# Sparse attention before a bilinear feed-forward: from half-array to whole-array matmuls on TensorE

## The chip, the cores and the metric

One core of a Trainium2 chip. The time is device microseconds of that core; "before" and "after" are the two kernels, each run several times. Profiled spans are about 1 to 2 us shorter than the timed runs. In the views PE is TensorE, PEld its weight loads, DVE VectorE, ACT ScalarE and POOL GpSimd; PSUM holds TensorE's results.

## The reference, cut to what matters

```python
B, H, S, D = 8, 8, 576, 64
scores = q @ k.T / 8                       # per batch and head
mask_local   = (0 <= i - j) & (i - j < 32)              # heads 0..3
mask_strided = (0 <= i - j) & (i % 32 == j % 32)        # heads 4..7
attn = softmax(where(mask, scores, -1e9))
x = (attn @ v).transpose(0, 2, 1, 3).reshape(4608, 512)
out = ((x @ w_a) * (x @ w_b)) @ w_out      # d_ff = 1536
```

## The kernel before

The feed-forward takes the tokens in 9 tiles of 512. A tile is 16 groups: 12 of `ffn_ab` (8 matmuls of 512 columns each) and 4 of `ffn_y` (12 each). The attention of batch 0 comes first; the attention of batch t+1 is cut into slots, one behind each group of tile t. An attention matmul uses half of the array, by rows or by columns, and two stand side by side. The steps of a batch have short names: T transposes q and k of a pair of heads (Tq and Tk apart in the kernel after), S makes scores, exp and mask, V is P times v, and X, in the kernel after alone, transposes x. The number is the pair for T and X (0 to 3), and half of a pair's queries for S and V (0 to 7).

```python
# transposes: two heads, each into half of the columns
for r in range(R):
    for hh in range(2):
        nc.tensor.transpose(tp[64*hh:64*hh+64, r, :], src[:, 2*cc+hh, r, :], ident[:n, :n])
# scores: each head in half of the rows
nc.tensor.matmul(st[:M, hh, i*n:(i+1)*n], lhsT=kT[d0:d0+64, c, k0:k0+M], rhs=qT[d0:d0+64, c, q0:q0+n], ...)
# denominators by ones, P times v, each head in half of the columns
nc.tensor.matmul(dn[64*hh:64*hh+64, :W], lhsT=ones[:M], rhs=p[:M, hh], ...)
nc.tensor.matmul(o[64*hh:64*hh+64, i*n:(i+1)*n], lhsT=vt, rhs=p[:M, hh, i*n:(i+1)*n], ...)
nc.scalar.activation(ln, dn[:, :W], ACT.Ln)
nc.scalar.activation(rc, ln, ACT.Exp, scale=-1.0)
nc.vector.tensor_mul(x[...], o[:, :W], rc)       # written straight into xT
# ... (cut)
```

TensorE's, GpSimd's and the DMA queue's order is the program's; ACT's and VectorE's order is made by a scheduler.

The softmax here doesn't subtract the row's maximum and nothing guards it: scores larger than these inputs give would overflow.

## Time and profile before

| | before |
|---|---|
| time, median | 375.7 us (375.3 to 376.4) |
| profiled span | 374.7 us |
| first feed-forward matmul | 25.21 us |
| tile 0 (with batch 1's attention) | 42.56 us |
| a later tile with attention | 39.95 us |
| the last tile, without | 31.08 us |

The times of tiles are differences between the starts of their first feed-forward matmuls. Read TensorE's order of time first: it carries 93% of the chain that ended last, so every microsecond of it is in the time. The prediction below shows those lines. One line that it does not show is of use later. It is from TensorE's timeline at the start of tile 1; the bracket says how long the engine had been idle and who ended that:

```profile
69.36 0.38 PE L254 MATMUL mm<-xT,wa_sb 128*128 128x512 bf16 x1 [0.77 <-DVE xT L232]
```

Three matmuls of that group start at 67.77 and the fourth should follow at 68.42; it starts 0.94 us late, since x's last quarter was late.

### The profile page before, as it was taken

To read this page: it belongs to the slowest core of one execution; us is meant where nothing else is said; L and a number is where in the kernel's file an instruction comes from. 1 tells how busy PE (TensorE), PEld (TensorE's weight loads), DVE (VectorE), ACT (ScalarE), POOL (GpSimd) and SP (SyncE) were. 2 spreads that over 40 slices of the span, in tenths; PEclk is the share of its full clock that TensorE was granted. 3 is DMA by queue.
4 is the path that set the end of the run, shared out by engine and by line. 5 is a ranking of instruction groups with operands and counts; after the bars stand their busy time and mean duration, and the time that the engine had idled before them with its cause. 6 is when DMAs were issued, how large, how long until landed. Compare 5 with 4: busy or idle time off the path is not lost.

```text
span 374.7 us, 7708 instructions
## 1 busy us (share of the span) xinstructions
PE 358.7 (96%) x3217; PEld 173.8 (46%) x3217; DVE 169.7 (45%) x299; ACT 178.6 (48%) x347; POOL 52.3 (14%) x72
## 2 busy tenths in 40 slices
PE   2789999999999999999999999999999999999995
PEld 2544454455444544444444544554445444444442
DVE  2653652465426652556245643655255513312421
ACT  1563764466526652666246643766166623312320
POOL 7833540013001110103000300000000000000000
PEclk9999999999999999999999999999999999999999
DMA  7999999845644194229414843000200020011002
GB/s 114 155 194 197 205 191 191 177 66 37 98 117 65 8 100 117 53 40 103 93 56 66 72 81 99 2 2 19 94 2 3 1 86 28 0 58 56 0 30 84
DMA packets 51730, 29.59 MB, mean 79 GB/s; under 512 B 28400, under 2 KB 47088, under 8 KB 51696
## 3 DMA queue, kind: packets, MB, share of 16 engines
q0 software_dynamic: 46512, 19.67, 43.2%
q1 hardware_dynamic: 5184, 9.44, 6.9%
q8 instruction: 25, 0.41, 0.4%
q14 instruction: 9, 0.07, 0.1%
HBM read 39.31 MB, written 9.44 MB: 130 GB/s over the span
## 4 chain that ended last, share of the span: by engine, by line
PE 93%; DMA 2%; POOL 1%; ACT 1%; DVE 1%; issue 1%; DVEq 0%; POOLq 0%
PE mm L254 52%; PE mm L265 25%; PE sm L166 5%; PE st L194 4%; PE sm L213 4%; PE sm L220 2%; DMA vl<-in_v_dram 2%; POOL k L116 0%; DVE y_sb L271 0%; POOL msl L73 0%; ACT rc L226 0%; DVE xT L232 0%; ACT ln L224 0%; POOL q L116 0%; PE mm L166 0%
## 5 line engine op out<-in xcount | busy, mean ns | idle before, releaser
L259 DVE TENSOR_TENSOR pf<-a_sb,mm 128x512 bf16<-128x512 f32 x108 | 74.3, 688 | 89.9 <-PE mm L254 89.9
L254 PE MATMUL mm<-xT,wa_sb 128*128 128x512 bf16 x432 | 113.6, 386 | 0.8 <-DVE xT L232 0.8
L254 PE MATMUL mm<-xT,wb_sb 128*128 128x512 bf16 x432 | 111.9, 382 | 0.0
L258 ACT COPY a_sb<-mm 128x512 f32<-128x512 f32 x108 | 63.2, 585 | 70.2 <-PE mm L254 70.2
L265 PE MATMUL mm<-wo_sb,pf 128*128 128x512 bf16 x432 | 96.3, 379 | 0.0
L254 PEld LDWEIGHTS <-wb_sb 128*128 128x128 bf16 x432 | 42.6, 99 | 52.9 <-issue 2.9
L265 PEld LDWEIGHTS <-pf 128*128 128x128 bf16 x432 | 40.9, 98 | 47.9
L254 PEld LDWEIGHTS <-wa_sb 128*128 128x128 bf16 x432 | 36.4, 98 | 38.4 <-issue 1.7
L199 ACT ACTIVATE p<-st 128x576 bf16<-128x576 f32 (+1 forms) x64 | 40.7, 635 | 17.5 <-PE st L194 17.4
L224 ACT ACTIVATE ln<-sm 128x288 f32<-128x288 f32 x64 | 26.3, 410 | 29.5 <-PE sm L213 29.5
L269 ACT COPY y_sb<-mm 128x512 f32<-128x512 f32 x18 | 10.5, 585 | 56.3 <-PE mm L265 56.3
L271 DVE COPY y_sb<-mm 128x512 f32<-128x512 f32 x18 | 12.5, 692 | 52.9 <-PE mm L265 52.9
L232 DVE TENSOR_TENSOR xT<-sm,rc 128x288 bf16<-128x288 f32 x32 | 20.4, 639 | 28.4 <-ACT rc L226 27.8
L226 ACT ACTIVATE rc<-ln 128x288 f32<-128x288 f32 x64 | 28.3, 443 | 2.0
L172 ACT COPY qT<-sm 128x576 bf16<-128x576 bf16 x28 | 17.8, 637 | 13.9 <-PE sm L166 13.9
L194 PE MATMUL st<-qT,kT 64*72 64x72 bf16 (+1 forms) x448 | 21.1, 212 | 0.6 <-ACT p L199 0.5
L213 PE MATMUL sm<-p,ones 72*64 72x288 bf16 (+1 forms) x128 | 21.1, 327 | 0.3 <-DVE p L205 0.3
L229 DVE TENSOR_TENSOR xT<-sm,rc 128x288 bf16<-128x288 f32 x32 | 14.6, 458 | 14.2 <-ACT rc L226 12.5
L116 POOL DMA_DIRECT2D q<-in_q_dram x16 | 11.7, 730 | 58.4 <-PE sm L166 53.7
L213 PEld LDWEIGHTS <-ones 72*64 72x64 bf16 (+1 forms) x128 | 7.3, 110 | 24.6 <-issue 21.2
L166 PEld LDWEIGHTS <-q 72*64 72x64 bf16 (+1 forms) x448 | 11.2, 117 | 15.9 <-issue 8.9
L129 POOL DMA_DIRECT2D vl<-in_v_dram x8 | 11.6, 1454 | 45.9 <-PE st L194 45.4
(41 smaller groups left out, 177.8 us busy)
## 6 DMA issues: line engine op xcount, KB each, us to landing
out_dram<-y_sb SPq DMA_DIRECT2D x36, 256.0 KB, 2.0
q<-in_q_dram POOLq DMA_DIRECT2D x16, 288.0 KB, 6.8
k<-in_k_dram POOLq DMA_DIRECT2D x16, 288.0 KB, 7.9
vl<-in_v_dram POOLq DMA_DIRECT2D x7, 384.0 KB, 6.8
vs<-in_v_dram POOLq DMA_DIRECT2D x8, 288.0 KB, 5.8
wa_sb<-in_moe_w_a_dram POOLq DMA_DIRECT2D x4, 384.0 KB, 11.6
wb_sb<-in_moe_w_b_dram POOLq DMA_DIRECT2D x4, 384.0 KB, 11.7
wo_sb<-in_moe_w_out_dram POOLq DMA_DIRECT2D x4, 384.0 KB, 13.5
```

The lines of the kernel that those rows point to most:

```text
L166: nc.tensor.transpose(tp[64 * hh:64 * hh + 64, r, :], src[:, 2 * cc + hh, r, :], ident[:n, :n])
L172: nc.scalar.copy(o, i_)
L194: nc.tensor.matmul(st[:M, hh, i * n:(i + 1) * n], lhsT=kT[d0:d0 + 64, c, k0:k0 + M], rhs=qT[d0:d0 + 64, c, q0:q0 + n], start=True, stop=True)
L199: nc.scalar.activation(p[:M], st[:M, :, :W], ACT.Exp, scale=scale)
L213: nc.tensor.matmul(dn[64 * hh:64 * hh + 64, :W], lhsT=ones[:M], rhs=p[:M, hh], start=True, stop=True)
L224: nc.scalar.activation(ln, dn[:, :W], ACT.Ln)
L226: nc.scalar.activation(rc, ln, ACT.Exp, scale=-1.0)
L232: nc.vector.tensor_mul(dst, o[:, :W].rearrange("d (r p) -> d p r", r=4), rc.rearrange("d (r p) -> d p r", r=4))
L254: nc.tensor.matmul(ps_, lhsT=w[:, f // FC, kk, 128 * (f % FC):128 * (f % FC + 1)], rhs=xT[:, kk, TTOK * t:TTOK * (t + 1)], start=(kk == 0) ...
L258: nc.scalar.copy(a_sb, ab[0])
L259: nc.vector.tensor_mul(pf[:, f, :], a_sb, ab[1])
L265: nc.tensor.matmul(y, lhsT=pf[:, f, 128 * j:128 * (j + 1)], rhs=wo_sb[:, f, :], start=(f == 0), stop=(f == FD - 1))
```

## The change

Its intent: leave the array whole, so that it need not change its shape. k is loaded for both heads of a pair over 128 rows, and q stands in two tiles with the other head's half zeroed. P becomes the loaded operand, read 128 columns wide, and v with a 65th column of ones the moving one, so that the denominators come along and x comes out with queries on the partitions; it must then be transposed on TensorE. Local q and k are regrouped by GpSimd so that one transpose takes two heads (from batch 2 on).

```diff
-            for hh in range(2):
-                nc.tensor.transpose(tp[64*hh:64*hh+64, r, :], src[:, 2*cc+hh, r, :], ident[:n, :n])
+            nc.tensor.transpose(tv[:, r, :], perm_t[b, nm][:, r, 2*c:2*c+2, :], ident[:96, :96])   # b > 1
-                nc.scalar.copy(o, i_)
+            for j in range(2):
+                nc.scalar.copy(perm(qz_buf[b % 2][j][pr, c, :]), tv[pr])     # pr: half of the partitions
-    lhsT=kT[d0:d0+64, c, k0:k0+M], rhs=qT[d0:d0+64, c, q0:q0+n]
+    lhsT=kT[:, c, k0:k0+M],        rhs=qz[j][:, c, q0:q0+n]
-    dn: lhsT=ones[:M], rhs=p[:M, hh];  o: lhsT=vt, rhs=p[:M, hh, i*n:(i+1)*n];  Ln, Exp(-1), mul
+    o: lhsT=p[:M, j, i*n:i*n+128], rhs=vt   # 65 columns
+    nc.vector.reciprocal(rc, ov[:, :, :, D]);  nc.vector.tensor_mul(xn, ov[..., 0:D], rc)
+    def step_X(b, c):  # transposes of xn, nc.scalar.copy into xT
+    def perm_qk(b):
+        nc.gpsimd.tensor_copy(t.rearrange("p r h d -> p h r d"), nats[b, nm, False])
-pmm 4 banks, psm 2, pst 2
+pmm 3 banks, po 2 (one tile), ptp 1 (one tile), pst 2 (one tile)
+batch b's slots begin two groups before tile b-1; batch 1's begin after group 2 of tile 0,
+with two slots behind groups 3 and 12 (Tq0 then S0,Tk1; S6 then S7,X2)
# ... (cut: order of loads, clearing of buffers, last y in halves)
```

## The prediction

> **What bounds the kernel now.** I read the page first (engine shares, chain of work that ended last, costliest groups), then the timeline of TensorE in three stretches, then the sums over windows.
>
> ```profile
> PE 358.7 (96%) x3217; PEld 173.8 (46%) x3217; DVE 169.7 (45%) x299; ACT 178.6 (48%) x347; POOL 52.3 (14%) x72
> PE mm L254 52%; PE mm L265 25%; PE sm L166 5%; PE st L194 4%; PE sm L213 4%; PE sm L220 2%; DMA vl<-in_v_dram 2%; POOL k L116 0%; DVE y_sb L271 0%; POOL msl L73 0%; ACT rc L226 0%; DVE xT L232 0%; ACT ln L224 0%; POOL q L116 0%; PE mm L166 0%
> ```
>
> TensorE carries 93% of the chain, and no other engine is half busy. So I read TensorE's own order. One feed-forward group, one attention slot, a group, a slot:
>
> ```profile
> 156.70 1.03 PE L254 MATMUL mm<-xT,wb_sb 128*128 128x512 bf16 x4
> 157.66 0.31 PE L213 MATMUL sm<-p,ones 128*64 128x288 bf16 x2
> 157.80 0.29 PE L220 MATMUL sm<-p,vl 128*64 128x96 bf16 x6
> 158.03 0.30 PE L194 MATMUL st<-qT,kT 64*128 64x96 bf16 x6
> 158.26 1.04 PE L254 MATMUL mm<-xT,wa_sb 128*128 128x512 bf16 x4
> ...
> 162.53 0.45 PE L166 MATMUL sm<-ident,q 72*64 72x72 bf16 x16
> 162.81 0.43 PE L166 MATMUL sm<-ident,k 72*64 72x72 bf16 x16
> 163.18 1.04 PE L254 MATMUL mm<-xT,wa_sb 128*128 128x512 bf16 x4
> ```
>
> The first number is the start of a group, so differences of starts are what a group costs. In the last tile, which has no attention, feed-forward groups run back to back:
>
> ```profile
> 339.50 1.03 PE L254 MATMUL mm<-xT,wa_sb 128*128 128x512 bf16 x4
> ...
> 360.22 10.52 PE L265 MATMUL mm<-wo_sb,pf 128*128 128x512 bf16 x48
> ```
>
> That is 20.72 us for 96 matmuls, 215.8 ns each, so a tile of 144 costs 31.08 us. A tile with attention takes 39.95 us:
>
> ```profile
> 150.43:190.38 39.95, 39.95 (x385) 19.29 (x385) 19.57 (x34) 21.42 (x42) 4.98 (x6) 1.00 0.51 74
> ```
>
> Attention therefore costs 8.87 us of TensorE per batch, and that is what the change can shorten. Its anatomy: a group of four wb_sb matmuls starts at 156.70 and should be through at 157.56, but the slot starts at 157.66: 0.10 us lost. From 158.03 three pairs of 96 columns should take 3 x 0.0425 = 0.13 us, yet the feed-forward resumes 0.23 us later: 0.10 lost again; between 157.80 and 158.03 once more. Each loss falls where the array's shape changes (128\*128, 128\*64, 64\*128). The sequence of one batch has 33 such changes (2 for a slot of one kind of work, 3 for a slot of two): 33 x 0.10 = 3.3 us. The rest, 5.5 us, is streaming, in which two half-array matmuls run beside each other.
>
> The start is another stage: the first feed-forward matmul is at 25.21 us, after a wait for v, and four matmuls there start 1.70 us apart from the next four instead of 0.86.
>
> ```profile
> 14.00 0.45 PE L220 MATMUL sm<-p,vl 128*64 128x96 bf16 x5 [1.81 <-DMA vl<-in_v_dram]
> ...
> 25.21 1.89 PE L254 MATMUL mm<-xT,wa_sb 128*128 128x512 bf16 x4
> 26.89 1.91 PE L254 MATMUL mm<-xT,wb_sb 128*128 128x512 bf16 x4
> ```
>
> **What the Trainium skill says.** (1) "TensorEngine Tiling (Array Packing)", Key Properties: changing the tiling mode drains TensorE. The trace agrees: about 0.10 us per change. (2) "TensorE: Matmul & The Clock Gate", Back-to-back issue gap: N/2.4 + 2.5 ns when warm. That is 215.8 for N=512, exactly the trace; the transposes at N=72 (16 in 0.28 us, two abreast) give 35 ns a pair against 32.5. But the same section has about 81 ns per matmul at N=128 for streams of load and matmul, which no group of before can test in the whole array. (3) Same page, Weight-path perf modes: the fast weight load wants 128 columns. The trace has 98 ns for loads of 128 columns and 115 to 117 for 64, so this agrees in direction. (4) Same page, Part 1: the array runs at half rate until it has been busy for a window. The 1.70 against 0.86 us agrees.
>
> **The change part by part.**
>
> *Whole-array attention, steady state.* After the change each matmul of batches 2 to 7 uses more than 64 rows and 65 or more stationary columns, so no shape changes: minus 3.3 us a batch. In exchange nothing runs two abreast. Per batch, by (2): 24 full local transposes x 42.5 ns = 1.02; 32 strided x 32.5 = 1.04; scores 24 x 42.5 + 32 x 35 (72-wide weights, no fast load; before shows 35 a pair) = 2.14; P times v now has P stationary, 56 x 29.6 (N=65) = 1.66, and its 65th column replaces the denominators' 16 matmuls of 288 columns; new transposes of x 12 x 42.5 + 16 x 32.5 = 1.03. Sum 6.89 us against 8.87: 2.0 saved, in six batches 11.9 us. Batch 1 keeps half-width local transposes with 8 shape changes (0.8): about 7.7, saved 1.2.
>
> *Other engines.* ACT loses ln and exp(-ln) (64 x 410 and 443 ns, 6.8 us a batch), gains the q copies in halves (8 x about 0.64, for 4 x 0.637) and 4 x copies. DVE loses no large thing and gains small reciprocals; its multiplications have about the old size. I sum about 21 us each per 38: neither is the bound. All of it lies beside TensorE. Following the slots by hand: q transpose, two ACT copies (1.3 us), then scores after one 1.73 us group, fits by 0.2 us; one PSUM tile for o, freed by reciprocal and multiply about 0.9 us later, fits in a group; three PSUM tiles instead of four for a and b leave over 1 us of slack. One pf buffer costs nothing, as its readers come before the next writer in TensorE's order anyway.
>
> *GpSimd.* Two copies of 96x1536 a batch, from batch 2. I assume a few us each (an estimate; before has none to measure). They depend on loads and on the previous batch's transposes, a dozen slots before their use, and delay only later DMA issues. Hidden.
>
> *Batch 1 in tile 0.* Two slots are doubled: scores right after their q transpose (wait for two ACT copies, 1.4 us) and S7 right after S6 with one st tile (0.9 us). Against that, before loses about 0.8 + 0.8 us at 67.8 to 69.4 (ACT and DVE finish x late), and after should lose 0.3 there. Net cost 1.0.
>
> *Start.* k lands at 7.6 us as before. Then the cold array: full-array work costs N/1.2, about 12.7 us in batch 0, and the chain is longer per step: scores wait for two ACT copies of q instead of a DVE copy, x goes through transposes and copies at the end. By hand, with the durations of before (exp 0.64, mask 0.46, copy 0.64, semaphore and fill 0.2), I get the first scores at 9.6, V0 at 12.2 (the v wait is gone, its load is earlier), S4 at 18.9, S6 at 23.2, V7 at 26.6 and feed-forward at about 28.3: 3.1 us later than 25.2.
>
> *Tail.* The last y in halves: a copy of 256 columns and half the DMA, 0.2 us saved.
>
> Sum: -11.9 - 1.2 + 1.0 + 3.1 - 0.2 = -9.2; I add 0.5 for small stalls: -8.7. Of 375.8 that leaves about 367; I put it at 366, since a denser batch 0 might wake the clock earlier (up to 3 us to win).
>
> **The rivals.**
>
> *A. Whole-array pairs of load and matmul don't stream at N/2.4.* If a load can't hide behind a 30 ns matmul, each pair has a floor. At 40 ns: 196 matmuls give 8.0 us, the gain is 0.9 a batch, total about 373. At the 81 ns of (2), 15.9 us a batch, total near 420. Against: in the transposes of before each column tile takes a new load and matmul every 33 to 35 ns, and the feed-forward hides full-width loads wholly.
>
> *B. Single PSUM tiles turn into waits.* One st, one o, one tp in a fixed slot order; if an ACT or DVE step slips by 0.3 us, TensorE waits in several slots: 0.5 to 1.5 us a batch, total 370 to 376. For: the q path has 0.2 us of slack. Against: both engines are some 55% loaded.
>
> *C. GpSimd's copies are late, or disturb VectorE.* If a copy took over 10 us, local transposes would wait; 2 us a batch, total 378. Against: they can start long before.
>
> *D. The start gains instead.* v is no longer waited for (1.8 us), and if the array warms early feed-forward starts near 25: total about 361.
>
> **Range and chances.** The streaming arithmetic is firm to about 0.5 us a batch (3.5 us), the start to 3 us, stalls only add. That gives 360 to 371. Faster by over 2% means below 368.3, just above my value; D and the fact that no step of the steady state lacks slack weigh for it, A and B against: 0.70 faster, 0.27 same, 0.03 slower.
>
> **What the new profile would show.** The period from one batch's slot to the same slot of the next should be 37.9 to 38.2 us; groups of attention should follow feed-forward without the 0.10 us gap; six matmuls of N=65 should start 0.18 us ahead of what follows; eight transposes of N=72, 0.26. First feed-forward matmul near 28 us. TensorE should wait for ACT twice in batch 1 and hardly elsewhere. Wrong would be: 45 ns or more per small matmul (A), waits of TensorE on copies in every batch (B), waits for kp or qp (C), a start beyond 30 us or before 26 (then the start, not the slots, moves the total).

## The result, and the profile after

The time is 371.15 us (370.95 to 371.2) against 375.7: ratio 0.9876, 95% interval 0.9859 to 0.9893. Ratios here are the mean time of one kernel's fast runs over that of the other's of the same rounds, so not quite the ratio of the medians. The change gains 1.2%, in the class "same" and just above the predicted range of 360 to 371.

The shares and the chain of the profile after:

```profile
PE 348.7 (94%) x2925; PEld 190.7 (52%) x2925; DVE 188.9 (51%) x369; ACT 174.3 (47%) x288; POOL 90.8 (25%) x108
PE 91%; ACT 3%; DVE 2%; DMA 1%; issue 1%; POOL 0%; DVEq 0%; POOLq 0%
```

TensorE still sets the end, but ACT and DVE now stand in the chain with 5% together. The averages do not tell where. In the steady state TensorE's timeline (start, duration, group) shows the changed slot:

```profile
157.52 1.03 PE L315 MATMUL mm<-xT,wb_sb 128*128 128x512 bf16 x4
158.38 0.34 PE L253 MATMUL o<-vl,p 128*128 128x65 bf16 x6
158.56 0.42 PE L227 MATMUL st<-qz,kT 128*128 128x96 bf16 x6
158.82 1.03 PE L315 MATMUL mm<-xT,wa_sb 128*128 128x512 bf16 x4
...
160.98 0.43 PE L195 MATMUL tp<-ident,k 72*128 72x72 bf16 x8
161.24 1.03 PE L315 MATMUL mm<-xT,wa_sb 128*128 128x512 bf16 x4
```

The attention follows the feed-forward at once (157.52 + 4 x 0.216 = 158.38), six matmuls of 65 columns take 0.18 us, six of 96 take 0.26, eight of 72 take 0.26. That is the predicted rate. The sums over windows give a tile of

```profile
152.17:190.22 38.05, 38.05 (x344) 21.00 (x342) 21.77 (x42) 20.55 (x34) 10.56 (x11) 1.00 0.60 78
```

38.05 us against 39.95. From 77 us to the end the profile lists no wait of TensorE (it lists those over 0.15 us). So what is missing was lost before that. The starts of the tiles give the balance:

| stretch | before | after | difference |
|---|---|---|---|
| to the first feed-forward matmul | 25.21 | 29.51 | +4.30 |
| tile 0 | 42.56 | 46.55 | +3.99 |
| tiles 1 to 6 | 240.65 | 227.81 | -12.84 |
| tiles 7, 8 and the end | 66.30 | 65.62 | -0.68 |
| span | 374.72 | 369.50 | -5.23 |

In tiles 1 to 6 are six periods' gains (6 x 1.90 = 11.4), before's wait of 0.94, and 0.5 for two slots of batch 2 that now stand in tile 0. The last row is the split last y and the copy and store behind it. For tile 0, the waits below are 4.4 us and the two slots of batch 2 are 0.5, so that batch 1's attention itself became about 0.9 cheaper (3.99 - 4.4 - 0.5).

TensorE's waits in tile 0 after the change, from its timeline:

```profile
40.87 0.20 PE L227 MATMUL st<-qz,kT 128*128 128x96 bf16 x1 [0.72 <-ACT qz L203]
41.53 0.37 PE L227 MATMUL st<-qz,kT 128*128 128x96 bf16 x5 [0.46 <-ACT qz L203]
...
61.11 0.42 PE L253 MATMUL o<-vs,p 72*128 72x65 bf16 x8 [0.83 <-DVE xn L264]
...
65.60 0.44 PE L227 MATMUL st<-qz,kT 128*72 128x72 bf16 x8 [0.94 <-ACT p L230]
...
75.81 0.41 PE L185 MATMUL tp<-ident,qp 96*128 96x96 bf16 x6 [0.73 <-ACT xT L281]
```

Counted from when each could have started, they lose 0.8 + 0.6, 1.0, 1.1 and 0.9 us: 4.4 in all. The first and the third belong to the doubled slots. The second is a surprise. All engines around it, in order of time:

```profile
56.43 1.48 POOL L141 COPY qp<-q 96x1536 bf16<-96x1536 bf16 x1
56.50 0.45 DVE L199 COPY kT<-tp 128x576 bf16<-128x576 bf16 x1
56.87 2.76 DVE L236 TENSOR_TENSOR p<-p,mask_s 72x576 int16<-72x576 int16 x1
57.84 1.47 POOL L141 COPY kp<-k 96x1536 bf16<-96x1536 bf16 x1
59.55 0.67 DVE L320 TENSOR_TENSOR pf<-a_sb,mm 128x512 bf16<-128x512 f32 x1
60.14 0.19 DVE L256 RECIPROCAL rc<-o 72x8 f32<-72x8 f32 x1
```

A mask operation that elsewhere takes 0.45 us took 2.76: it began during the first GpSimd copy and ended at 59.63, 0.33 us after the second. VectorE's next operations came behind it, so the reciprocal of V4 came at 60.14 instead of about 58.8 (0.88 us after its group, as in the run in pieces below), behind the delayed pf product (the product of the feed-forward's two halves), and V5 waited for its PSUM tile. The kT copy, which reads PSUM, took 0.45 us beside the first GpSimd copy; a pf product, with one input in PSUM, took its usual 0.69 us beside a GpSimd copy at 82.95. The Trainium skill, "SBUF — State Buffer", section Who interferes with whom, says that a VectorE instruction with two SBUF inputs contends with a GpSimd instruction that reads SBUF, and the page's summary that the second of the two to issue is blocked until the first is through. The mask's wait for the first copy fits that; its wait for the second, which began after the mask, isn't stated there.

### The profile page after: what moved, and what is told of

It is laid out like the page before. It is cut to its first block, busy times and chain, and to the rows that moved or that the text cites. A ratio compares the mean times of both kernels' runs of the same rounds, so it can differ in the third digit from the quotient of the medians.

```text
span 369.5 us, 7057 instructions
## 1 busy us (share of the span) xinstructions
PE 348.7 (94%) x2925; PEld 190.7 (52%) x2925; DVE 188.9 (51%) x369; ACT 174.3 (47%) x288; POOL 90.8 (25%) x108
## 4 chain that ended last, share of the span: by engine, by line
PE 91%; ACT 3%; DVE 2%; DMA 1%; issue 1%; POOL 0%; DVEq 0%; POOLq 0%
PE mm L315 50%; PE mm L329 25%; PE st L227 5%; PE o L253 4%; PE tp L195 2%; PE tp L275 2%; ACT qz L203 2%; PE tp L185 2%; DMA k<-in_k_dram 1%; DVE xn L264 1%; ACT p L230 1%; DVE p L236 1%; PE mm L275 0%; PE tp L188 0%; DVE pf L320 0%
## 5 line engine op out<-in xcount | busy, mean ns | idle before, releaser
L329 PE MATMUL mm<-wo_sb,pf 128*128 128x512 bf16 (+1 forms) x444 | 98.1, 373 | 0.0
L203 ACT COPY qz<-tp 64x576 bf16<-64x576 bf16 x56 | 35.3, 631 | 26.0 <-PE tp L185 13.1
L264 DVE TENSOR_TENSOR xn<-o,rc 96x384 bf16<-96x384 f32 (+1 forms) x64 | 39.6, 619 | 1.9
L157 POOL DMA_DIRECT2D vs<-in_v_dram x32 | 25.9, 812 | 35.8 <-PE o L253 24.5
L227 PE MATMUL st<-qz,kT 128*72 128x72 bf16 (+1 forms) x448 | 29.9, 210 | 5.0 <-ACT qz L203 3.1
L335 DVE COPY y_sb<-mm 128x512 f32<-128x512 f32 (+1 forms) x18 | 12.2, 676 | 43.9 <-PE mm L329 43.9
L227 PEld LDWEIGHTS <-kT 128*72 128x72 bf16 (+1 forms) x448 | 25.8, 114 | 13.5 <-issue 5.6
L253 PEld LDWEIGHTS <-p 72*128 72x128 bf16 (+1 forms) x448 | 22.6, 101 | 17.6 <-DVE xn L264 5.3
L281 ACT COPY xT<-tp 128x576 bf16<-128x576 bf16 x28 | 17.7, 631 | 23.3 <-PE tp L275 23.3
L199 DVE COPY kT<-tp 128x576 bf16<-128x576 bf16 x28 | 16.6, 592 | 13.9 <-PE tp L185 12.1
L236 DVE TENSOR_TENSOR p<-p,mask_l 128x576 int16<-128x576 int16 x32 | 19.3, 604 | 3.7 <-ACT p L230 3.7
```

The lines of the kernel that those rows point to most:

```text
L157: nc.gpsimd.dma_start(out=vs_buf[b % 2][:, h, :, 0:D], in_=v[b, HL + h].rearrange("(p r) d -> p r d", r=RS))
L203: nc.scalar.copy(perm(qz_buf[b % 2][j][pr, c, :]), tv[pr])
L227: nc.tensor.matmul(st[:M, j, i * n:(i + 1) * n], lhsT=kT[:, c, k0:k0 + M], rhs=qz[j][:, c, q0:q0 + n], start=True, stop=True)
L236: nc.vector.tensor_tensor(pi, pi, mk, op=ALU.bitwise_and)
L253: nc.tensor.matmul(of[:, j, i, :], lhsT=p[:M, j, i * n:i * n + 128], rhs=vt, start=True, stop=True)
L264: nc.vector.tensor_mul(dst, ov[:, :, :, 0:D], rc[:n, :, :G].unsqueeze(3).to_broadcast([n, 2, G, D]))
```

## The experiments

The theory after reading: the slots gained what was forecast; 4.3 us were lost in batch 0 and 3.4 net in tile 0. The rivals are those in the expectations. "Changed kernel" is the one after; it is 371.15 us in its own rounds and 370.9 in a control. Each kernel's page and trace were compared with it, since two things vary by themselves. One is the half-rate phase, from the first feed-forward matmul to the trace's record of full clock: 5.5 and 5.8 us in two profiles of the changed kernel. The other is V5's wait: TensorE idle for 0.83 and 0.45 us before it.

One trap has to be taken out first. Of all profiles, only before and after hold the record of the first feed-forward matmul. The control of the same kernel shows it: after the same last transposes at 29.04 us, one profile lists four matmuls of wa_sb from 29.51 us on, the other three from 29.92, and in both wb_sb follows at 31.20.

```profile
29.51 1.90 PE L315 MATMUL mm<-xT,wa_sb 128*128 128x512 bf16 x4
```

```profile
29.92 1.49 PE L315 MATMUL mm<-xT,wa_sb 128*128 128x512 bf16 x3 [0.22 <-issue]
```

So a start that the other profiles list is 0.43 us late (one matmul at half rate), and a tile 1 whose first record is missing 0.22 late. The starts and tiles below are corrected for that; the expectations aren't.

### The changed kernel again

No edit.

> The changed kernel once more, as a control beside the last two: 371.0 to 371.3 us as before if chips agree, the spread of single runs within 0.5 us.

Measured: 370.9 us (370.87 to 370.97, and one run of 368.64), before 376.4, ratio 0.9839 [0.9803, 0.9876]. The median agrees; the spread did not. A difference of a microsecond in a single run says nothing here.

### Undo the regrouping

```diff
-                if b > 1:          # transposes from perm_t
+                if b > B:          # never; all batches by halves
-            loads[g0 + 11] = lambda b=b: (load_vs(b), perm_qk(b))
+            loads[g0 + 11] = lambda b=b: load_vs(b)
```

> The regrouping by GpSimd is undone: batches 2 to 7 also transpose local q and k by halves of the array, as batch 1 does, and GpSimd copies nothing; the rest is the changed kernel. Theory (a change of the array's shape costs about 0.10 us, 8 of them come back per batch, while the halves stream two abreast): the period of a tile rises from 38.05 to about 38.85 us, six batches give 4.8 us more, of which 1.0 us comes back because the mask operation before V5 of batch 1 is no longer held up: total about 375, with all mask operations near 0.45 us. Rival (shape changes next to transposes are free, or the regrouping costs what it saves): period unchanged, total 370 to 371.

Measured: 374.63 us, ratio 0.9957 [0.9935, 0.998]. The period of a tile is 38.95 us, 0.89 more for eight changes of shape: 0.11 us each, or 0.10 if the 0.02 us by which twelve half transposes stream longer than six whole ones is taken off four times. TensorE's timeline in a slot with scores and half transposes:

```profile
155.00 0.42 PE L227 MATMUL st<-qz,kT 128*128 128x96 bf16 x6
155.35 0.45 PE L188 MATMUL tp<-ident,k 96*64 96x96 bf16 x12
155.73 1.04 PE L315 MATMUL mm<-xT,wa_sb 128*128 128x512 bf16 x4
```

Six scores take 0.35 us before a half transpose, against 0.26 before a whole-array group. All mask operations are near 0.45 us again. The theory's two numbers hold, so the regrouping is worth 3.5 to 3.7 us of the total, although its copies hold up VectorE. With no copies, V5 doesn't wait.

### P read as wide as there are queries

```diff
-lhsT=p[:M, j, i*n:i*n+128]     # out: of[:, j, i, :]
+lhsT=p[:M, j, i*n:i*n+n]       # out: of[:n, j, i, :]
```

> P is read 96 or 72 columns wide, as many as there are queries, instead of 128; all else is the changed kernel. Theory (loads of 128 columns are the quick ones, 101 ns in the trace against 114 to 124 for 72 columns, and a narrow load no longer hides behind a matmul of 65 columns): P times v takes 40 ns per local matmul and 32 to 35 per strided one instead of 30, 0.3 to 0.4 us per batch, total 2 to 3 us more, some 373.5. Rival (the load hides anyway, the width does nothing): P times v keeps 0.18 and 0.24 us per slot and the total stays at 371.2.

Measured: 373.72 us, ratio 0.9943 [0.9917, 0.9969]; the period is 38.49 us, 0.43 more, which is 2.6 in six. The groups of loads by form, of this kernel and then of the changed one (busy us, mean ns of one):

```profile
L253 PEld LDWEIGHTS <-p 128*96 128x96 bf16 x192 | 14.2, 133 | 7.5 <-DVE xn L264 2.7
```

```profile
L253 PEld LDWEIGHTS <-p 128*128 128x128 bf16 x192 | 10.0, 101 | 8.6 <-DVE xn L264 3.3
```

A load of 96 columns is slower than one of 128. In the timeline of this kernel

```profile
158.98 0.42 PE L253 MATMUL o<-vl,p 128*96 128x65 bf16 x6
159.23 0.42 PE L227 MATMUL st<-qz,kT 128*128 128x96 bf16 x6
```

six matmuls take 0.25 us, 42 ns each against 30: the load no longer hides behind 65 columns. Eight strided ones, read 72 wide, take 0.28 us instead of 0.24. Reading columns that nobody needs buys 2.6 to 2.8 us.

### GpSimd's copies in six pieces

```diff
-nc.gpsimd.tensor_copy(t.rearrange("p r h d -> p h r d"), nats[b, nm, False])
+for r in range(RL):
+    nc.gpsimd.tensor_copy(t[:, r], nats[b, nm, False][:, :, r, :])
```

> GpSimd's regrouping is done in six small copies per tensor instead of one. Theory (VectorE's mask operation, which took 2.76 us at 56.9 us and 1.45 us once in each later batch while a GpSimd copy ran, against 0.45 us otherwise, waits for the end of the running GpSimd instruction): its worst case falls to about 0.45 plus one small copy (0.3 to 0.7 us more), the wait of TensorE before V5 of batch 1 (0.99 us) goes, total about 0.8 us less, some 370.3; nothing changes in later batches, which have no waits. Rival (the two share bandwidth rather than take turns): the mask operations still take 1.4 us or more beside the copies and the time stays at 371.2.

Measured: 369.16 us, ratio 0.9822 [0.9802, 0.9842]. The timeline of all engines at the same place:

```profile
55.49 0.55 DVE L237 TENSOR_TENSOR p<-p,mask_s 72x576 int16<-72x576 int16 x1
56.03 2.10 POOL L142 COPY qp<-q 96x256 bf16<-96x256 bf16 x6
...
58.74 0.41 PE L254 MATMUL o<-vs,p 72*128 72x65 bf16 x8
```

No mask operation of the whole run exceeds 0.6 us, though GpSimd copies longer in all (12 pieces of 0.45 us against 2 of 1.56 per batch). In later batches, where the copies run beside the mask, it falls from 1.45 to under 0.6 us, and the period stays 38.05: there it had been off the path. In tile 0 V5 follows its group without a wait (57.88 + 0.86 = 58.74), but this isn't the pieces' doing alone, if at all: TensorE was ahead, and the mask was over at 56.04, when the first piece began at 56.03. The combined run below has a mask amid the pieces in tile 0, and it takes 0.67 us:

```profile
55.32 2.32 POOL L143 COPY qp<-q 96x256 bf16<-96x256 bf16 x6
56.72 0.67 DVE L309 TENSOR_TENSOR p<-p,mask_s 72x576 int16<-72x576 int16 x1
```

The gain of 2 us is more than the 1.0 of the wait; in this profile the half-rate phase lasted 2.8 us instead of 5.5, which is worth 1.3 in the profile, and was not the edit's aim. One run of the unedited control, 368.64 us, is as fast, so the clock doesn't show what the edit gains.

### Batch 1 from the first group, no doubled slots

```diff
-todo.append((b, 2 if b == 1 else 16 * (b - 1) - 2, ...))
+todo.append((b, 0 if b == 1 else 16 * (b - 1) - 2, ...))
-                    if b == 1 and i in (3, 12):
-                        run(b, seq.pop(0))
```

> Batch 1's attention begins after the first feed-forward group instead of the third, one slot per group, no doubled slot. Theory (what was lost in tile 0 is TensorE waiting inside the doubled slots: 1.4 us before S0 and 1.1 us before the second S7 scores in the trace): both waits go, about 2.5 us less than the changed kernel, some 368.7. Rival 1 (the waits only move, because the data of batch 1 arrives late in the first groups): new waits on DMA, gain under 1 us. Rival 2 (the tile is bound by ACT or DVE, not by these two slots): no gain.

Measured: 367.21 us, ratio 0.9766 [0.9751, 0.9781]. Tile 0 falls from 46.55 to 42.71 us. No wait on DMA appears, and none before S0, S7 or V5. Of the 3.84 us, 2.5 are the doubled slots and 1.0 is V5's, because batch 2's GpSimd copies no longer meet a mask operation; the first that is held up comes at 77.2 us, in tile 1, where it does no harm. The half-rate phase of 5.0 instead of 5.5 us is worth about the rest.

### The last transpose of x of batch 1 in another PSUM tile

```diff
-        if b == 0:
+        if b == 0 or (b == 1 and c == 3):
             tp = pmm.tile([128, S], BF16, tag="mm", name="mm")
```

> The last transpose of x of batch 1 goes through a PSUM tile of the feed-forward's pool, all else is the changed kernel. Theory (batch 2's q transpose waits 0.73 to 0.89 us at 75.8 us because it shares the single tile with that transpose, whose copy ACT must finish): this wait goes, 0.3 us of it may come back as the first group of tile 1 waits for x itself; total 0.5 to 0.9 us less. Rival (the feed-forward's pool, short of a tile, passes the wait on): no gain.

Measured: 370.13 us, ratio 0.9841 [0.9822, 0.9859], against 370.9 for the control of the same rounds. In the timeline the wait is gone:

```profile
74.11 0.43 PE L275 MATMUL mm<-ident,xn 72*128 72x72 bf16 x8
74.37 0.42 PE L185 MATMUL tp<-ident,qp 96*128 96x96 bf16 x6
74.63 1.03 PE L315 MATMUL mm<-xT,wa_sb 128*128 128x512 bf16 x3
```

Tile 1 took 38.10 us. The time difference of 0.8 is about that of the theory, but smaller than the spread of the control, the ratios are the same, and a half-rate phase of 4.4 instead of 5.5 us would give 0.5 of it; the timeline carries the verdict, not the clock.

### q's two copies of batch 0 on two engines

```diff
-                nc.scalar.copy(perm(qz_buf[b % 2][j][pr, c, :]), tv[pr])
+                (nc.vector.tensor_copy if b == 0 and j == 1 else nc.scalar.copy)(...)
```

> In batch 0 alone the two half copies of q go to ACT and DVE side by side instead of one after the other on ACT. Theory (the late start of the feed-forward, 29.5 us against 25.2, comes from the chain of copies between q's transposes and the scores, which TensorE waits for at 9.5, 10.2, 19.4, 22.7 and 23.4 us, about 2 us in all): the first feed-forward matmul comes 1.3 to 1.9 us earlier, the time falls as much, to about 369.6. Rival (the cold array's whole-width streaming binds the start): under 0.5 us.

Measured: 370.89 us, ratio 0.9868 [0.985, 0.9886]. The first feed-forward matmul came at 29.83 us, not earlier. But the edit didn't do what it was meant to: the two copies never ran side by side. The first pair, on both engines:

```profile
8.94 0.63 ACT L206 COPY qz<-mm 64x576 bf16<-64x576 bf16 x1 [6.85 <-PE mm L188]
9.61 0.76 DVE L204 COPY qz<-mm 64x576 bf16<-64x576 bf16 x1 [0.39 <-ACT qz L206]
```

In all four pairs VectorE's copy began after ACT's had ended, and in two VectorE had sat idle until then (0.39 and 0.59 us); in the last it also stood behind a multiplication. TensorE now waits for VectorE's copies for 1.9 us and for ACT's for 1.8, where it was 3.1 for ACT's alone. Why the copies took turns isn't shown, so this run tests neither the theory nor the rival.

### Batch 0 as in the kernel before

```diff
-        for slot in ("Tk0", "Tq0", "Tk1", "S0", "Tq1", "S1"):
-            run(0, (slot,))
+        for slot in ("T0", "T1", "S0"):
+            OLD[slot[0]](int(slot[1]))      # half-array steps, dn in ptp, o in po
# ... (cut: the rest of batch 0 alike: S1 T2 V0 S2 V1 S3 T3 V2 S4 ... V7)
```

> Batch 0 alone is computed as in the kernel before (half-array transposes, scores and P times v, ln and exp for the denominators, x written without a transpose), all later batches as in the changed kernel, the earlier load of v kept. Theory (of the lost time 4.3 us lie in batch 0's longer chain): the first feed-forward matmul comes at 24 to 25.5 us, total 366 to 367. Rival (the start is late because loads come in another order or VectorE clears the q buffers first, not because of the attention steps): first feed-forward matmul stays after 27 us, gain under 2 us.

Measured: 368.49 us with runs from 366.6 to 369.9, ratio 0.9808 [0.9762, 0.9854], unclear by its spread; the feed-forward starts at 26.85 us, between the two expectations. TensorE waited 2.4 us for a mask matrix that GpSimd, now busy with loads, built late. So the trial was mended: `ef = mask_strided()` before the strided loads.

> Batch 0 as in the kernel before, again, with GpSimd building the small mask matrix before it issues the strided loads; in the first trial TensorE waited 2.4 us for that matrix. Theory (the lost time of the start is the longer chain of batch 0): first feed-forward matmul at 24.5 to 25.5 us, 4 to 5 us before the changed kernel, total 365.5 to 367, a spread between runs of some us included, as the clock's warm-up falls differently. Rival (the loads, not the chain): still after 27 us.

Measured: 367.44 us with runs from 366.5 to 370.0, ratio 0.978 [0.9739, 0.9821], again unclear; start 27.29 us, where the rival had it. The expectation failed again: with the mask out of the way, TensorE waited for the strided q and k, which are loaded after v now, while the old order of slots wants them before. It is settled by the last experiment below.

### Everything together

```diff
# batch 0 old with the mask first + batch 1 early + six pieces + other tile for X3
```

> Everything found so far together: batch 0 as before with the mask matrix first, batch 1's slots from the first feed-forward group on, GpSimd's copies in six pieces, and the last transpose of x of batch 1 in a PSUM tile of the feed-forward's pool, so that batch 2's q transpose needn't wait for its copy. Theory (the losses before the second tile simply add: 4.5 start, 2.5 doubled slots, 1.0 held-up mask, 0.6 shared tile): 371.2 - 8.6, some 362.5. Rival (with an earlier start batch 1's data isn't there yet): TensorE waits for DMA in tile 0, 364 to 367.

Measured: 363.75 us, ratio 0.9673 [0.965, 0.9696]. Tile 0 takes 40.76 us, without a wait on DMA in it; the start is again late, 27.25 us, with waits of 1.6 and 1.5 us for the strided loads. Tile 0 lost 5.8 us: the 4.4 of its waits, which are all gone, and the rest by a half-rate phase of 2.6 us. The start was still out of step with the loads.

### The same, strided transposes later

```diff
-("S1", "T2", "V0", "S2", "V1", "S3", "T3", "V2", "S4", "V3", "S5", "V4", ...)
+("S1", "V0", "S2", "V1", "S3", "V2", "T2", "S4", "V3", "T3", "S5", "V4", ...)
```

> As the last combined kernel, but batch 0's strided transposes stand after the local P times v steps, since the trace showed TensorE waiting 1.6 and 1.5 us for the strided loads, which come later now than v. Theory (with the loads in step, the steps of the kernel before need only 24 to 25 us to the first feed-forward matmul, so that the changed batch 0 is some 4.5 us longer by its own chain): start 24 to 25.5 us, total 360 to 361.5. Rival (batch 0 is bound by its V steps, each waiting for the one PSUM tile of o): start stays above 26.5 us, total 362.5 or more.

Measured: 361.63 us (361.44 to 362.23), ratio 0.9616 [0.9598, 0.9634]: 3.8% better than before, and 2.5% better than the changed kernel by the medians of the same rounds (361.63 / 370.9). Its timeline at the start, with the first feed-forward record missing:

```profile
24.15 0.45 PE L262 MATMUL o<-p,vs 72*64 72x72 bf16 x8 [0.50 <-DVE xT L273]
24.94 1.49 PE L388 MATMUL mm<-xT,wa_sb 128*128 128x512 bf16 x3 [0.33 <-issue]
```

Half-array steps reach the feed-forward at 24.51 us where the changed batch 0 needs 29.5, with the same loads in nearly the same order. The difference of 5.0 us is that of the attention steps and the two placed orders; the theory had 4.5. Part of it is lost again in tile 0, where TensorE now waits 0.85 us for batch 1's k, at 28.85 us: what the rival of the run before had feared. What share of it is the half-rate array streaming whole-width work and what the chain of copies, no run here separates.

## Why the prediction was right or wrong

**Steady state: right.** Forecast 6.89 us of attention per batch, measured 38.05 - 31.08 = 6.97; the forecast period of 37.9 to 38.2 holds. The shape changes cost 0.10 to 0.11 us each, as undoing the regrouping shows, and small loads and matmuls stream at the forecast rate. Rival A (a floor of 40 ns or more per pair) is refuted: 30 ns at 65 columns. It becomes true with a narrow load, 42 ns.

**Where it failed: "Batch 1 in tile 0 ... Net cost 1.0".** It was 3.4: 4.4 us of waits after less 0.94 before. Four corrections make that up, less the 0.3 that it allowed for x at the start of tile 1. The two doubled slots cost 2.5 rather than 2.3. Before's own wait, deducted as 1.6, was 0.94 by TensorE's starts. The mask held up by GpSimd, 1.0, was missing: "GpSimd ... Hidden", and rival C had "disturb VectorE" in its title but argued lateness alone. And batch 2's q transpose waits 0.9 for the single tp tile, which is rival B's wait, once instead of in every batch; I had followed the slots within a batch, not where two batches meet.

**Mis-sized: "Start".** Forecast 28.3 us, measured 29.51; forecast 3.1 us later, measured 4.3. Until S6 the working by hand holds (V0 forecast 12.2, measured 12.42; S4 18.9 and 18.70; S6 23.2 and 22.69), although V1 came late, at 15.07: VectorE's scheduled order put the second mask, which waited for an exp, before V0's reciprocal. The step that failed is the end of the chain, from S6 on. V7 came at 27.40 instead of 26.6: V6 waited 0.45 us for its mask, which VectorE ran behind V5's multiplication, and V7 waited 0.54 for V6's multiplication. From V7 to the feed-forward it took 2.11 us instead of 1.7. The durations were right (exp 0.65, mask 0.45, copy 0.64); which link was missed in the working by hand isn't on record.

**The hope for an earlier warm clock** (from 367 down to 366) was not a step of the sum and did not come: the half-rate phase lasted 5.3 us before and 5.5 after.

**The tail** gained 0.7 rather than 0.2.

Put together: 367, plus 2.4 for the waits of tile 0, 0.3 for batch 1 (0.9 saved instead of 1.2), 1.2 for the start, 0.5 for six times 0.08 us, less 0.5 for the tail, is 370.9, against 371.15 measured; the 367 has the prediction's 0.5 for small stalls in it. The mechanism was right where it runs six times; the sum failed where it runs once.

The chances (0.70 for faster by over 2%) followed from a value that lay just below the threshold; with these terms it lies above.

## What to carry to other kernels

Before pricing a change by its steady state, list what happens once, the first batch, the first tile and the seam between two batches, and read there each engine's order as well as each duration; here 13.5 us were won from tile 1 on and 8.3 lost in the first 76 us. A change need not be applied to every stage: the half-array steps were the better ones for the first batch, the whole-array steps where TensorE is always busy, and the best kernel has both. And an operation moved to an idle GpSimd was not free for a VectorE instruction with two SBUF inputs (2.76 us instead of 0.45); in small pieces it cost that instruction 0.1 to 0.2 us.

## What the Trainium skill lacked or had wrong

- "TensorEngine Tiling (Array Packing)", Key Properties, says that a change of mode drains TensorE but not what that costs: 0.10 us per change in the kernel before, 0.11 by undoing the regrouping (0.89 us for eight).
- "TensorE: Matmul & The Clock Gate", Back-to-back issue gap, gives about 81 ns per matmul at N=128 and about 131 at N=512 for streams of load and matmul. Here the feed-forward, with a new load for each matmul, takes 215.8 ns at N=512, and whole-array pairs take 30 ns at N=65, about 33 at N=72 and 43 at N=96. N/2.4 + 2.5, which the section gives for a single matmul, fits all four; the 131 doesn't hold here, and N=128 was not run.
- The same page, Weight-path perf modes, doesn't say when a load of under 128 columns stops hiding: 96 columns behind a matmul of 65 give 42 ns instead of 30.
- "SBUF — State Buffer", Who interferes with whom, agrees with the held-up mask. It doesn't tell that one VectorE instruction can wait through two queued GpSimd instructions: 2.76 us at 56.87 us, past the end of the second copy, while in later batches it waited for one (1.45 us). Why the two cases differ is open.
- Nothing was lacking on the half-rate start, but the view misleads: it prints a granted clock of 1.00 from the start on, while the first feed-forward matmuls run at half rate (four in 1.70 us instead of 0.86). The trace's clock table begins only with the record of full clock, at 30.53 us before and 34.99 after, which is where the half rate ends; the 1.00 until then isn't a measurement.
